# Transposing q by one crossbar DMA a batch, from batch 2 on, in a fused attention and GEGLU kernel

## The chip, the cores and the metric

One core of one Trainium2 chip. The metric is the device time of one execution in microseconds, the median over the runs named. Single executions of one kernel mostly agree within 0.2%, so differences of 0.5 us need several runs and a look at the trace.

## The reference, cut to what matters

```python
# q, k, v: (8 batches, 8 heads, 576 rows, 64); float32
q_s = softmax(q, axis=-1)            # over the 64 channels of a head
k_s = softmax(k, axis=2)             # over the 576 rows
kv  = einsum('bhsd,bhse->bhde', k_s, v)
x   = einsum('bhsd,bhde->bhse', q_s, kv)      # -> (4608 rows, 512 channels)
out = (gelu(x @ w_gate) * (x @ w_val)) @ w_out     # 512 -> 1536 -> 512
```

## The kernel before

Rows are worked in nine blocks: for each batch a block of 512 rows, and one more block of the 8 x 64 remainder rows. A block is twelve FFN tiles `FI` 0 to 11 (four matmuls for the gate, psg; four for the value, psv; gelu on ScalarE; the product ht on VectorE) and four row blocks `NS` 0 to 3 (twelve matmuls into psy each, then evacuation and store). The attention of batch b+1 rides along in block b: a plan says after which tile each piece is issued. In the program each engine has one list of instructions, worked in order (in run 9 VectorE stood 6.01 us at a sum with an evacuation, ready to run, behind it).

Names: eq and ek are the exp of q and k; q3 is q of batch 3, and so on. psg, psv, psy, psx, pst, pstr and pskv are the tiles in PSUM that TensorE writes: gate, value, output, x, transposes of the 512 rows and of the remainder rows, and kv. A bank is the place of one such tile; ps_big has six, ps_att two. The SP queue is SyncE's list of DMAs, issued one after the other (after the change: one from 69.56 us for 3.19, the next at 72.81). The chain is the profile's "chain of work that ended last", followed back from the last instruction.

For x = q_s · kv, the kernel's matmuls take q_s with channels on the partitions (`psx<-eqt,kv` in the trace). The kernel before makes that transpose in two ways. Batches 0 to 2: TensorE transposes into PSUM (8 transposes step by 0.50 us when nothing waits) and VectorE copies it out (0.68 us). Batches 3 to 7: VectorE transposes, in the 32x32 blocks of the code below (0.845 us a call), and 16 small DMAs move the blocks to their partitions (10.66 us of the SP queue in block 2).

```python
ps_big = tile_pool(name="ps_big", bufs=6, PSUM)    # psg, psv, psy, psx
ps_att = tile_pool(name="ps_att", bufs=2, PSUM)    # attention pieces
...
def unit_t(b, g, eng="dve"):                       # batches 0 to 2, twice a batch
    pst = ps_att.tile([P, 2, MAIN], f16, name="pst", tag="att")
    ... 8 x nc.tensor.transpose(pst[...], eq_b[b % 2][...], ident)
    ... copy to eqt on VectorE
def unit_t32(b, hp):                               # batches 3 to 7, four times a batch
    nc.vector.transpose(out=et[...], in_=eq_b[b % 2][...])
def moves(b):
    for a in range(4):
        for c in range(4):
            nc.sync.dma_start(out=t[32*c:32*c+32, a], in_=et[32*a:32*a+32, c])
...
at(1, FI, 3, L(exp, "q", 2), L(norm, 2, 0))        # softmax of q, batch 2
at(1, FI, 4, L(norm, 2, 1), L(unit_xrem, 1))
at(1, FI, 5, L(norm, 2, 2))
at(1, FI, 6, L(norm, 2, 3))
at(1, FI, 7, L(exp, "k", 2, 0, 4), L(cast_v, 2, 0, H))
at(1, FI, 9, L(unit_t, 2, 0))
at(1, FI, 10, L(unit_t, 2, 1))
at(1, FI, 11, L(load_batch, 3), L(exp, "k", 2, 4, 8), L(exp, "q", 3), L(exp, "k", 3), ...)
at(1, NS, 0, L(unit_trem, 2))                      # 4 more transposes: remainder rows
at(1, NS, 1, L(unit_kv4, 2))
at(1, NS, 2, L(unit_x4, 2, ("dve", "dve")))
```

The softmax here doesn't subtract the row's maximum and nothing guards it: scores larger than these inputs give would overflow.

## Time and profile before

| | before |
|---|---|
| time, median of 4 runs | 316.15 us (315.94 to 316.39) |
| span of the profiled execution | 314.5 us |
| TensorE / VectorE / ScalarE / GpSimd busy | 98 / 61 / 44 / 14% |
| start of block 2 on the chain | 85.42 us |
| length of blocks 2 and 3 | 33.42 and 32.89 us |

How to read it: matmuls overlap in the records (four 512-column ones are recorded as 1.03 us and start 0.86 us apart when nothing waits), so distances between starts are what to go by. The lines of TensorE in block 1 and of the chain are shown in the prediction.

### The profile page before, as it was taken

The page shows a single profiled execution, that of the slowest core. Times are in us where ns is not written, and L with a number is a line of the kernel's source. Part 1 is how long each engine was busy: PE and PEld are TensorE (multiplying, and loading weights), DVE is VectorE, ACT ScalarE, POOL GpSimd, SP SyncE. Part 2 cuts the span into 40 slices and gives each one's busy share as a digit, 9 for nine tenths or more (in the row PEclk, how much of TensorE's full clock was granted, in tenths as well). Part 3 has the DMA queues.
Part 4 walks back from the last instruction along what each step waited for, and adds up shares of the span by engine and source line. Part 5 has one row for each costly group of instructions (what it writes and reads, how often), then busy time and mean ns, then how long its engine had stood idle before and what let it go on. Part 6 is the DMA issues. An engine that isn't in the chain of part 4 may idle for free.

```text
span 314.5 us, 4799 instructions
## 1 busy us (share of the span) xinstructions
PE 307.7 (98%) x1826; PEld 143.7 (46%) x1826; DVE 191.1 (61%) x324; ACT 138.5 (44%) x178; POOL 44.7 (14%) x59
## 2 busy tenths in 40 slices
PE   8899999999999999999999999999999999999995
PEld 3444454444444444444444444444444444444443
DVE  3844386597898479746984599458943434324331
ACT  3753564988433663356334643374330233013300
POOL 2657451331001200030003000300000000000000
PEclk9999999999999999999999999999999999999999
DMA  7999999950178116921492139303021200140002
GB/s 231 372 383 394 401 386 388 395 194 0 69 245 306 53 70 194 349 59 67 127 386 80 72 90 383 115 27 131 1 58 28 115 18 0 35 101 0 3 33 100
DMA packets 42343, 50.78 MB, mean 161 GB/s; under 512 B 3408, under 2 KB 38096, under 8 KB 42320
## 3 DMA queue, kind: packets, MB, share of 16 engines
q1 hardware_dynamic: 40592, 48.84, 45.0%
q10 hardware_dynamic: 1728, 1.64, 1.6%
q8 instruction: 14, 0.23, 0.3%
q14 instruction: 9, 0.07, 0.1%
HBM read 37.75 MB, written 9.44 MB: 150 GB/s over the span
## 4 chain that ended last, share of the span: by engine, by line
PE 90%; DVE 4%; DMA 2%; ACT 2%; issue 1%; ACTq 0%; DVEq 0%
PE psy L489 29%; PE psg L411 28%; PE psv L411 27%; DMA qt<-in_q_dram 2%; PE pskv L284 1%; DVE eq L200 1%; PE psl L510 1%; PE psx L383 1%; DVE rq L191 1%; DVE rq L181 1%; DVE ht L418 1%; PE psx L365 1%; ACT eq L163 1%; PE pst L306 1%; ACT L416 0%
## 5 line engine op out<-in xcount | busy, mean ns | idle before, releaser
L416 ACT ACTIVATE gl<-psg 128x512 f32<-128x512 f32 x108 | 64.0, 599 | 131.0 <-PE psg L411 124.5
L418 DVE SCALAR_TENSOR_TENSOR ht<-psv,gl 128x512 f16<-128x512 f32 x108 | 72.9, 682 | 64.6 <-PE psv L411 64.1
L411 PE MATMUL psg<-xt,wg_sb 128*128 128x512 f16 x384 | 100.5, 379 | 0.1
L411 PE MATMUL psv<-xt,wv_sb 128*128 128x512 f16 x384 | 100.5, 379 | 0.0
L489 PE MATMUL psy<-wo_sb,ht 128*128 128x512 f16 x420 | 94.0, 379 | 0.0
L411 PEld LDWEIGHTS <-wv_sb 128*128 128x128 f16 x432 | 42.3, 98 | 51.2 <-issue 0.8
L411 PEld LDWEIGHTS <-wg_sb 128*128 128x128 f16 x432 | 41.9, 98 | 49.4 <-issue 0.4
L489 PEld LDWEIGHTS <-ht 128*128 128x128 f16 x420 | 40.4, 98 | 47.9 <-issue 0.8
L538 DVE TENSOR_SCALAR yo<-psy 128x512 f32<-128x512 f32 x30 | 20.5, 685 | 29.7 <-PE psy L489 29.7
L139 POOL CAST v<-vt 128x640 f16<-128x640 f32 x26 | 18.8, 763 | 137.1 <-DMA vt<-in_v_dram 98.3
L181 DVE TENSOR_REDUCE rq<-eq 128x10 f32<-128x640 f16 x28 | 22.7, 812 | 6.1 <-ACT eq L163 5.7
L200 DVE TENSOR_TENSOR eq<-eq,rrq 128x640 f16<-128x640 f16 (+1 forms) x29 | 23.7, 817 | 0.3
L163 ACT ACTIVATE ek<-kt 128x1280 f16<-128x1280 f32 (+1 forms) x11 | 19.1, 1746 | 3.4 <-DMA kt<-in_k_dram 3.3
L163 ACT ACTIVATE eq<-qt 128x2560 f16<-128x2560 f32 (+2 forms) x10 | 18.4, 1863 | 2.3 <-DMA qt<-in_q_dram 2.2
L331 DVE STREAM_TRANSPOSE et<-eq 128x640 f16<-128x640 f16 x20 | 16.9, 845 | 0.7
L411 PE MATMUL psg<-xtr,wg_sb 128*128 128x512 f16 x48 | 12.3, 379 | 0.0
L411 PE MATMUL psv<-xtr,wv_sb 128*128 128x512 f16 x48 | 12.3, 379 | 0.0
L143 DVE CAST xt<-psx 128x512 f16<-128x512 f32 x16 | 10.2, 682 | 1.2 <-PE psx L365 1.2
L403 PE MATMUL pswarm<-warm,ident 128*128 128x512 f16 x34 | 9.5, 438 | 1.4 <-POOL ident masks.py:199 1.4
L163 ACT ACT_TABLE_LOAD x8 | 10.3, 1283 | 0.6 <-DMA qt<-in_q_dram 0.5
L141 ACT CAST xt<-psx 128x512 f16<-128x512 f32 x16 | 8.7, 588 | 3.5 <-PE psx L365 3.5
L141 ACT CAST xtr<-psxr 128x128 f16<-128x128 f32 (+1 forms) x6 | 1.7, 283 | 17.8 <-PE psxr L383 17.8
(74 smaller groups left out, 122.6 us busy)
## 6 DMA issues: line engine op xcount, KB each, us to landing
out_dram<-yo SPq DMA_DIRECT2D x14, 512.0 KB, 3.5
kt<-in_k_dram SPq DMA_DIRECT2D x7, 640.0 KB, 7.9
vt<-in_v_dram SPq DMA_DIRECT2D x7, 640.0 KB, 8.4
qt<-in_q_dram SPq DMA_DIRECT2D x7, 640.0 KB, 6.5
qt<-in_q_dram SPq DMA_DIRECT2D x8, 512.0 KB, 6.7
eqt<-et SPq DMA_DIRECT2D x80, 40.0 KB, 1.9
wost<-in_moe_w_out_dram SPq DMA_DIRECT2D x6, 512.0 KB, 7.9
kt<-in_k_dram SPq DMA_DIRECT2D x6, 512.0 KB, 8.1
```

The source lines that it names most:

```text
L139: nc.gpsimd.tensor_copy(out=dst, in_=src)
L141: nc.scalar.copy(out=dst, in_=src)
L143: nc.vector.tensor_copy(out=dst, in_=src)
L163: nc.scalar.activation(out=dst[:, n0:NC, h0 * D:h1 * D].rearrange(o, d=D, **({"t": 2} if b >= QUAD else {})), in_=heads(tiles[(nm, b)], b, ...
L181: nc.vector.reduce_sum(rq, e, axis=mybir.AxisListType.X)
L200: (nc.gpsimd if eng == "pool" else nc.vector).tensor_tensor(out=e, in0=e, in1=rrq.unsqueeze(-1).to_broadcast((P, n, 2, D)), op=ALU.mult)
L331: nc.vector.transpose(out=et[:, :, hp].rearrange("p c (n i) -> p n c i", i=32), in_=eq_b[b % 2][:, :, hp * P:(hp + 1) * P].rearrange("p n ...
L411: nc.tensor.matmul(ps, w[:, ci, fi * P:(fi + 1) * P], xt[:, ci, :], start=(ci == 0), stop=(ci == HP - 1))
L416: nc.scalar.activation(out=gl, in_=psg, func=ACTF.Gelu)
L418: nc.vector.scalar_tensor_tensor(out=ht, in0=psv, scalar=_H_SCALE, in1=gl, op0=ALU.mult, op1=ALU.mult)
L489: nc.tensor.matmul(psy, hts[fi][:, ns * P:(ns + 1) * P], wo_sb[:, fi, :], start=(fi == 0), stop=(fi == NFI - 1))
L538: nc.vector.tensor_scalar(out=yo, in0=psy, scalar1=1.0 / _H_SCALE, scalar2=None, op0=ALU.mult)
```

## The change

Intent: take the transposes of batch 2 off TensorE, and for all later batches drop VectorE's block transposes and the 16 moves; one crossbar DMA does each batch (only my name for a DMA that transposes while it copies: `dma_start_transpose` in the code, DMA_TRANSPOSE in the profile). To have q of batch 2 ready earlier, its four multiplies go to GpSimd. kv and x of batch 2 come one row block earlier. The sums of batch 3 move from block 1 into block 2. With ps_att no longer used by transposes, FFN tile 7 of block 1 takes its two banks.

```diff
-    def unit_t32(b, hp): ...
-    def moves(b): ...
+    def unit_td(b):
+        t = att.tile([P, NC * C], f16, name="eqt", tag="eqt").rearrange(
+            "p (n h t) -> p n h t", n=NC, h=HP)
+        nc.sync.dma_start_transpose(out=t.rearrange("p n h t -> p (n h) t"),
+                                    in_=eq_b[b % 2].rearrange("p n c -> p (n c)"))
+        st[(b, "eqt4")] = t
 ...
-    def ffn_fi(xt, fi):
-        psg = ps_big.tile([P, 512], f32, name="psg", tag="mm")
+    def ffn_fi(xt, fi, spare=False):
+        pool, tag = (ps_att, "att") if spare else (ps_big, "mm")
+        psg = pool.tile([P, 512], f32, name="psg", tag=tag)
 ...                                   # psv the same
-    at(1, FI, 3, L(exp, "q", 2), L(norm, 2, 0))
+    at(1, FI, 3, L(exp, "q", 2), L(norm, 2, 0, "pool"))
 ...                                   # "pool" for the other three as well
-    at(1, FI, 9, L(unit_t, 2, 0))
-    at(1, FI, 10, L(unit_t, 2, 1))
+    at(1, FI, 9, L(unit_td, 2))
 ...
-    at(1, NS, 0, L(unit_trem, 2))
-    at(1, NS, 1, L(unit_kv4, 2))
-    at(1, NS, 2, L(unit_x4, 2, ("dve", "dve")))
+    at(1, NS, 0, L(unit_kv4, 2))
+    at(1, NS, 1, L(unit_x4, 2, ("dve", "dve")))
 ...                                   # batches n = b + 1 = 3 to 7:
-                at(b - 1, NS, hp, L(norm_sum, n, hp))
-                at(b, FI, hp, L(norm_mul, n, hp), L(unit_t32, n, hp))
-            at(b, FI, 4, L(moves, n))
+                at(*((b, FI, hp) if n == 3 else (b - 1, NS, hp)), L(norm_sum, n, hp))
+                at(b, FI, hp, L(norm_mul, n, hp))
+            at(b, FI, 4, L(unit_td, n))
 ...
-            hts.append(ffn_fi(xt, fi))
+            hts.append(ffn_fi(xt, fi, b == 1 and fi == 7))
```

More of the change, by code (lines that the diff above doesn't have):

```diff
@@ L103 @@
     QUAD = 2
-    T32 = 3
     def heads(x, b, h0, h1):
@@ L122 @@
     wst = {}
-    ETW = HP * 4 * NC * 32
     def wst_tile(name, n, w):
-        t = wstp.tile([P, ETW], f16, name=name, tag="wst")
-        return t[:, 0:2 * n * w].bitcast(f32).rearrange("p (n w) -> p n w", n=n)
+        return wstp.tile([P, HP * 256], f32, name=name, tag="wst")[:, 0:n * w].rearrange(
+            "p (n w) -> p n w", n=n)
     def load_w_gv(c):
@@ L295, in get_eqt @@
         if (b, "eqt") not in st:
-            st[(b, "eqt")] = att.tile([P, HP * 4 * NC * 32], f16, name="eqt", tag="eqt")[
+            st[(b, "eqt")] = att.tile([P, NC * C], f16, name="eqt", tag="eqt")[
                 :, 0:HP * S].rearrange("p (h t) -> p h t", h=HP)
@@ L324, in unit_trem @@
         nc.vector.tensor_copy(out=st[(b, "eqtr")], in_=pst[:, :, 0:REM] if b == 0 else pst[:, :, 0:P:2])
-    def unit_t32(b, hp):
-        if (b, "et") not in st:
-            st[(b, "et")] = wstp.tile([P, 4, HP, NC * 32], f16, name="et", tag="wst")
-        et = st[(b, "et")]
-        nc.vector.transpose(
-            out=et[:, :, hp].rearrange("p c (n i) -> p n c i", i=32),
-            in_=eq_b[b % 2][:, :, hp * P:(hp + 1) * P].rearrange("p n (c j) -> p n c j", j=32))
-    def moves(b):
-        t = att.tile([P, HP * 4 * NC * 32], f16, name="eqt", tag="eqt").rearrange(
-            "p (a h x) -> p a h x", a=4, h=HP)
-        for a in range(4):
-            for c in range(4):
-                nc.sync.dma_start(out=t[32 * c:32 * c + 32, a],
-                                  in_=st[(b, "et")][32 * a:32 * a + 32, c])
-        t = t.rearrange("p a h (n i) -> p h n a i", i=32)
-        st[(b, "eqt5")] = t
+    def unit_td(b):
[4 more added lines that the diff above has]
+        st[(b, "eqt4")] = t
     def xq(b, hp):
-        if (b, "eqt5") in st:
-            return st[(b, "eqt5")][:, hp, 1:NC]
+        if (b, "eqt4") in st:
+            return st[(b, "eqt4")][:, 1:NC, hp]
         return st[(b, "eqt")][:, hp, 0:MAIN]
     def xqr(b, hp):
-        if (b, "eqt5") in st:
-            return st[(b, "eqt5")][:, hp, 0, :, 0:32:2]
+        if (b, "eqt4") in st:
+            return st[(b, "eqt4")][:, 0, hp, 0:P:2]
         return st[(b, "eqtr")][:, hp, :]
@@ L420, in gate @@
         return ht
-    def ffn_fi(xt, fi):
-        psg = ps_big.tile([P, 512], f32, name="psg", tag="mm")
+    def ffn_fi(xt, fi, spare=False):
+        pool, tag = (ps_att, "att") if spare else (ps_big, "mm")
+        psg = pool.tile([P, 512], f32, name="psg", tag=tag)
         mm_gv(psg, wg_sb, xt, fi, range(HP))
-        psv = ps_big.tile([P, 512], f32, name="psv", tag="mm")
+        psv = pool.tile([P, 512], f32, name="psv", tag=tag)
         mm_gv(psv, wv_sb, xt, fi, range(HP))
@@ L630 @@
     at(1, FI, 2, L(unit_trem, 1))
-    at(1, FI, 3, L(exp, "q", 2), L(norm, 2, 0))
-    at(1, FI, 4, L(norm, 2, 1), L(unit_xrem, 1))
-    at(1, FI, 5, L(norm, 2, 2))
-    at(1, FI, 6, L(norm, 2, 3))
+    at(1, FI, 3, L(exp, "q", 2), L(norm, 2, 0, "pool"))
+    at(1, FI, 4, L(norm, 2, 1, "pool"), L(unit_xrem, 1))
+    at(1, FI, 5, L(norm, 2, 2, "pool"))
+    at(1, FI, 6, L(norm, 2, 3, "pool"))
     at(1, FI, 7, L(exp, "k", 2, 0, 4), L(cast_v, 2, 0, H))
-    at(1, FI, 9, L(unit_t, 2, 0))
-    at(1, FI, 10, L(unit_t, 2, 1))
+    at(1, FI, 9, L(unit_td, 2))
     at(1, FI, 11, L(load_batch, 3), L(exp, "k", 2, 4, 8), L(exp, "q", 3), L(exp, "k", 3), L(exp_rem0), L(cast_v, 3, 0, H))
-    at(1, NS, 0, L(unit_trem, 2))
-    at(1, NS, 1, L(unit_kv4, 2))
-    at(1, NS, 2, L(unit_x4, 2, ("dve", "dve")))
+    at(1, NS, 0, L(unit_kv4, 2))
+    at(1, NS, 1, L(unit_x4, 2, ("dve", "dve")))
     at(2, FI, 7, L(norm_rem0))
@@ L651 @@
             for hp in range(HP):
-                at(b - 1, NS, hp, L(norm_sum, n, hp))
-                at(b, FI, hp, L(norm_mul, n, hp), L(unit_t32, n, hp))
-            at(b, FI, 4, L(moves, n))
-            if n == T32:
+                at(*((b, FI, hp) if n == 3 else (b - 1, NS, hp)), L(norm_sum, n, hp))
+                at(b, FI, hp, L(norm_mul, n, hp))
+            at(b, FI, 4, L(unit_td, n))
+            if n == 3:
                 at(b, FI, 5, L(unit_kv4, n))
```

## The prediction

The forecast's sum came to -1.72 + 1.1 = -0.6 us, 315.3 us. The transpose's time in the SP queue, 5 us, and its landing 1.5 us after that were my estimates, which no trace showed. The times reckoned from them: q3 and k3 issued at 74.6 us, k3 landed at 82.9, transposed q landed at 76.1, the first gelu of block 2 started at 87.3 and its ht ended at 88.5. That is 1.1 us after the 87.4 that the text allows: the 1.1 of the sum. The 2.5 and 8 us under "The range" are other values for the same SP time, a factor of two about 5.

> **What bounds the kernel now.** I read the page's first rows, then its chain of work that ended last, then that chain in order of time, then the timelines of TensorE, ScalarE and the SP queue through block 1, where the change acts.
>
> ```profile
> PE 307.7 (98%) x1826; PEld 143.7 (46%) x1826; DVE 191.1 (61%) x324; ACT 138.5 (44%) x178; POOL 44.7 (14%) x59
> ```
> ```profile
> PE 90%; DVE 4%; DMA 2%; ACT 2%; issue 1%; ACTq 0%; DVEq 0%
> ```
>
> TensorE is busy for 98% of the span and 90% of the chain, and the pieces of the chain show that this is true throughput, not only overlapped records: from block 2 on, each group of four 512-column matmuls takes 0.86 us and each 12-matmul row block 2.6 us, with no gap. Blocks 3, 4 and 5 start at 151.73, 184.29 and 216.85 us, 32.56 apart; 24 x 0.864 + 48 x 0.216 = 31.1 of that is the FFN, the rest the two attention pieces (kv 0.75, x 0.63). So VectorE's 191 us are worth nothing by themselves. Only TensorE instructions taken out, or TensorE waits taken away, can shorten this kernel. TensorE in block 1 (start us, duration us, line, output, count):
>
> ```profile
> 59.51 1.03 PE L411 MATMUL psg<-xt,wg_sb 128*128 128x512 f16 x4
> 60.38 1.03 PE L411 MATMUL psv<-xt,wv_sb 128*128 128x512 f16 x4
> 61.24 1.03 PE L411 MATMUL psg<-xt,wg_sb 128*128 128x512 f16 x4
> 62.10 1.03 PE L411 MATMUL psv<-xt,wv_sb 128*128 128x512 f16 x4
> 63.21 1.02 PE L411 MATMUL psg<-xt,wg_sb 128*128 128x512 f16 x4
> ...
> 68.39 0.61 PE L306 MATMUL pst<-ident,eq 128*128 128x128 f16 x8
> 68.89 1.02 PE L411 MATMUL psg<-xt,wg_sb 128*128 128x512 f16 x4
> 69.75 1.03 PE L411 MATMUL psv<-xt,wv_sb 128*128 128x512 f16 x4
> 70.61 0.92 PE L306 MATMUL pst<-ident,eq 128*128 128x128 f16 x8
> 71.36 1.03 PE L411 MATMUL psg<-xt,wg_sb 128*128 128x512 f16 x4
> ...
> 75.68 0.39 PE L320 MATMUL pstr<-ident,eq 128*128 128x128 f16 x4
> 75.90 2.75 PE L489 MATMUL psy<-wo_sb,ht 128*128 128x512 f16 x12
> ```
>
> Read the distances between starts. 62.10 to 63.21 is 1.11 where 0.86 is the rule: a wait of 0.25. The first eight transposes cost 0.50, the second eight 0.75 (with a wait of about 0.3 for the last normalisation on VectorE), the four remainder ones 0.22. The waits-for view names the former: pst for DVE eq, 0.4 us.
>
> The wait at 63.21 comes from ScalarE, which had its tables changed twice around the exp of q2:
>
> ```profile
> 58.92 2.34 ACT L163 ACTIVATE eq<-qt 128x2560 f16<-128x2560 f32 x1
> 61.27 1.28 ACT L416 ACT_TABLE_LOAD   x1
> 62.56 0.60 ACT L416 ACTIVATE gl<-psg 128x512 f32<-128x512 f32 x1
> ```
>
> Tile 4 frees its bank at 63.16, and tile 7, three tiles later, needs that one of the six banks.
>
> [...] The trace has plain loads at 385 to 400 GB/s, no transposes. [...] the multiply at 69.85 us took 1.23 instead of 0.82 us while GpSimd cast.
>
> **The change part by part.**
>
> *TensorE.* Out go 16 + 4 transposes of batch 2: 0.50 + 0.75 + 0.22 = 1.47 us of start-to-start time, the wait for the last normalisation included. The spare banks for tile 7 of block 1 take away the wait of 0.25. Sum: **1.72 us**, all on the path. Batches 3 to 7 had no TensorE transposes, so nothing more comes from there: blocks 2 to 7 should keep 32.56 us each.
>
> *VectorE.* Out go 20 block transposes (20 x 0.845 = 16.9 us), two evacuations of 0.68, one of 0.41 and four multiplies of 0.82 (to GpSimd): some 22 us, off the path, worth nothing except where they delayed something.
>
> *GpSimd.* Four multiplies of 128x640. The one that it already does took 1.26 us, so 5.0 us. The sums on VectorE pace them: exp of q2 ends at 61.26; sum and reciprocal take 1.07, with a gate (0.65) between, so the four sums end at about 62.4, 64.9, 66.6 and 68.3, and the last multiply at **69.6**. The casts of v2 (4 x 0.72, before at 58.17) follow and end at 72.5.
>
> *The SP queue.* 80 moves of about 0.66 us issue time go; six transposes of 640 KB come. [...] For batches 3 to 7 this replaces 10.7 us of moves (start 96.90 in block 2) in a stage with need at 114.70: off the path.
>
> *Where it is on the path.* Batch 2's transpose waits in the SP queue for 69.6. Behind it, in order, stand the loads of batch 3, which before went out as soon as the queue was free:
>
> ```profile
> 52.69 1.34 SPq L117 DMA_DIRECT2D qt<-in_q_dram  x2
> 54.07 3.52 SPq L117 DMA_DIRECT2D kt<-in_k_dram  x2
> 60.92 1.28 SPq L117 DMA_DIRECT2D vt<-in_v_dram  x2
> ```
>
> [...] In block 2 the same two loads, issued from 87.85 into an idle DMA, had moved their 2.6 MB by about 96.1 (summing the GB/s of the one-microsecond windows): 8.3 us. [...] ScalarE then does exp k3 (2.32), the remainder exp (0.61) and the table load (1.28), all ahead of block 2's first gate[...].
>
> TensorE, 1.72 earlier, starts block 2 at 85.26 - 1.72 = 83.5. With six banks it can run three tiles ahead. The binding reader is VectorE: the sums of batch 3 have moved into block 2, so its first four tiles cost ht 0.6 + sum 0.81 + reciprocal 0.22 + multiply 0.82 = 2.45 each, against TensorE's 1.73. ht of tile 4 then ends 9.8 after ht of tile 0, and psv of tile 7 needs its bank at 83.5 + 0.86 + 7 x 1.73 + 0.75 (kv of batch 3) = 97.2. So ht of tile 0 may end as late as 87.4 without a stall[...]. The stall grows one for one with the transpose's SP time above 3.9 us.
>
> The x matmuls of batch 2, moved one row block earlier, would start at 82.03 - 2.70 - 1.72 = 77.6[...]. exp of the second half of k2, before at 75.6 and now about 74.0, is in time for kv of batch 2 at about 74.2, by little.
>
> Sum: -1.72 + 1.1 = -0.6 us, **315.3**.
>
> **The rivals.** *A: the clean gain.* The transpose issues in under 4 us, nothing stalls: 315.99 - 1.72 = 314.3. For it: the change puts the x matmuls one row block earlier, which nobody does whose transpose comes late; and the DMA stands idle (0 GB/s) between 68 and 80 us. Against it: the order of the SP queue. *B: the late loads.* The SP queue holds q3, k3 back, ScalarE waits at their exps with block 2's gates behind it, and TensorE runs out of banks. With 9 us of issue time the stall is 5.1: 319.4. For it: the removal of batch 3's sums from block 1's row blocks, which is what one does when exp q3 comes late. *C: the transpose itself is slow,* ten or more us of landing; then x of batch 2 waits too. Both waits overlap (one delay shifts the other's deadline), so with 12 us I would expect 12 - 3.9 - 1.72 = +6.4: 322.4. [...] *D: the DMA transposes hold the loads of later batches:* 18 us of slack per block speak against it.
>
> **The range.** The floor is A with small extras, 314.1. [...] 2.5 gives A, 8 gives 315.99 - 1.72 + 4.1 = 318.4. That makes 314.1 to 318.4 for 8 in 10. Faster by 2% needs 6.3 us off; only 1.72 can be had: 0.01. Slower by 2% needs about 12 us of SP time: 0.06. Within: 0.93.
>
> **What would show it.** In the profile after: TensorE's block 1 without pst and pstr, all steps 0.86; the GpSimd multiplies near 1.26 us; the transpose issued at about 69.6 [...]; q3 and k3 issued after it; ScalarE waiting for the k3 DMA[...]; and how long TensorE stands still in tiles 3 to 7 of block 2. Blocks 3 to 7 must keep 32.56. I am wrong if the loads are not behind the transpose[...], or if the later blocks change length.

## The result, and the profile after

| | before | after |
|---|---|---|
| time, median of 4 runs | 316.15 us | 314.74 us (314.71 to 314.79) |
| ratio to before, 95% interval | | 0.9955 (0.9938 to 0.9973) |
| span of the profiled execution | 314.5 us | 312.8 us |
| TensorE busy, instructions | 307.7 us, 1826 | 306.0 us, 1806 |
| VectorE busy | 191.1 us | 171.7 us |
| start of block 2 on the chain | 85.42 us | 83.80 us |
| length of block 2 on the chain | 33.42 us | 33.42 us |

A ratio is the mean time of one kernel's runs over that of the other's of the same rounds, so not quite the ratio of the medians. Where runs of different calls are compared below, I compare their ratios to before, or their traces.

The change is 1.4 us (0.45%) faster. First the page of the kernel after: engines, and the chain by engine.

```profile
PE 306.0 (98%) x1806; PEld 142.5 (46%) x1806; DVE 171.7 (55%) x297; ACT 138.5 (44%) x178; POOL 48.6 (16%) x63
...
PE 94%; DVE 2%; DMA 2%; ACT 0%; issue 0%; ACTq 0%
```

TensorE's share of the chain rises from 90 to 94%; ScalarE's 2% falls to 0. TensorE's timeline in block 1 of the kernel after (start us, duration us, line, output, count):

```profile
62.20 1.03 PE L397 MATMUL psv<-xt,wv_sb 128*128 128x512 f16 x4
63.06 1.03 PE L397 MATMUL psg<-xt,wg_sb 128*128 128x512 f16 x4
...
69.10 1.03 PE L397 MATMUL psv<-xt,wv_sb 128*128 128x512 f16 x4
69.97 1.03 PE L397 MATMUL psg<-xt,wg_sb 128*128 128x512 f16 x4
...
77.83 0.26 PE L369 MATMUL psxr<-eqt,kv 64*64 64x64 f16 x8
```

The step into psg of tile 7 is 63.06 - 62.20 = 0.86, so the wait of 0.25 us is gone; between tiles 10 and 11 stands nothing. x of batch 2 starts at 77.83, where I had 77.6, and waits for nothing. Next the SP queue of the kernel after:

```profile
69.56 3.19 SPq L327 DMA_TRANSPOSE eqt<-eq  x1
72.81 1.29 SPq L116 DMA_DIRECT2D qt<-in_q_dram  x2
74.15 1.31 SPq L116 DMA_DIRECT2D kt<-in_k_dram  x2
```

The transpose issues at 69.56 (I had 69.6) and q3 and k3 do stand behind it; but it holds SP for 3.19 us, where my estimate was 5. ScalarE, which needs these loads, in the kernel before and after:

```profile
75.51 2.32 ACT L163 ACTIVATE eq<-qt 128x2560 f16<-128x2560 f32 x1
```
```profile
79.12 2.34 ACT L160 ACTIVATE eq<-qt 128x2560 f16<-128x2560 f32 x1 [4.91 <-DMA qt<-in_q_dram]
82.07 2.34 ACT L160 ACTIVATE ek<-kt 128x2560 f16<-128x2560 f32 x1 [0.61 <-DMA kt<-in_k_dram]
...
86.23 1.09 ACT L402 ACTIVATE gl<-psg 128x512 f32<-128x512 f32 x2
```

The new wait is real: 4.91 us for q3 and 0.61 for k3, where the kernel before had none. Block 2's first gelu starts at 86.23, which is 2.59 us after the block's first matmul (83.64), where before it was 1.06 (86.32 after 85.26). It costs nothing, for block 2 is as long as before.

### The profile page after: what moved, and what is told of

It reads as the page before. It is cut to its first block, busy times and chain, and to the rows that moved or that the text cites. A ratio compares the mean times of both kernels' runs of the same rounds, so it can differ in the third digit from the quotient of the medians.

```text
span 312.8 us, 4653 instructions
## 1 busy us (share of the span) xinstructions
PE 306.0 (98%) x1806; PEld 142.5 (46%) x1806; DVE 171.7 (55%) x297; ACT 138.5 (44%) x178; POOL 48.6 (16%) x63
## 4 chain that ended last, share of the span: by engine, by line
PE 94%; DVE 2%; DMA 2%; ACT 0%; issue 0%; ACTq 0%
PE psg L397 30%; PE psv L397 30%; PE psy L476 29%; DMA qt<-in_q_dram 2%; PE pskv L281 1%; PE psl L497 1%; PE psx L369 1%; DVE rq L188 1%; PE psx L351 1%; DVE eq L197 0%; PE pst L303 0%; PE pskv L224 0%; PE psxr L369 0%; ACT eq L160 0%; PE pskv L258 0%; DVE v L140 0%
## 5 line engine op out<-in xcount | busy, mean ns | idle before, releaser
L404 DVE SCALAR_TENSOR_TENSOR ht<-psv,gl 128x512 f16<-128x512 f32 x108 | 73.8, 689 | 79.5 <-PE psv L397 75.0
L136 POOL CAST v<-vt 128x640 f16<-128x640 f32 x26 | 17.7, 724 | 115.0 <-DMA vt<-in_v_dram 105.4
L197 DVE TENSOR_TENSOR eq<-eq,rrq 128x640 f16<-128x640 f16 (+1 forms) x25 | 20.3, 813 | 0.3
L197 POOL TENSOR_TENSOR eq<-eq,rrq 128x640 f16<-128x640 f16 (+1 forms) x7 | 9.3, 1323 | 25.0 <-DVE rrq L180 17.3
```

Of the source, the lines that this page charges most:

```text
L136: nc.gpsimd.tensor_copy(out=dst, in_=src)
L197: (nc.gpsimd if eng == "pool" else nc.vector).tensor_tensor(out=e, in0=e, in1=rrq.unsqueeze(-1).to_broadcast((P, n, 2, D)), op=ALU.mult)
L404: nc.vector.scalar_tensor_tensor(out=ht, in0=psv, scalar=_H_SCALE, in1=gl, op0=ALU.mult, op1=ALU.mult)
```

## The experiments

Twelve kernels ran, in four calls; each call measured the kernel before anew on its chip. All gave correct results. The ratio of the changed kernel, to compare with, is 0.9955.

**1. Without the spare banks** (changed kernel).

```diff
-            hts.append(ffn_fi(xt, fi, b == 1 and fi == 7))
+            hts.append(ffn_fi(xt, fi))
```

> The changed kernel with tile 7 of block 1 back in the six FFN banks. My theory (the gain is 1.47 us of TensorE transposes and their wait, plus 0.25 us of bank wait): the step before psg of tile 7 grows again from 0.86 to about 1.1 us, the later starts of block 1 move by that, and since the slack before block 2's stall is close to nil, the time is 0.25 us above the changed kernel: about 315.0. Rival (the bank wait was hidden, or is moved to a later tile that waits anyway): the changed kernel's 314.74.

Measured: 314.95 us, ratio 0.9957 (0.9944 to 0.9969). The times alone don't tell it from the changed kernel. The trace does: psg of tile 7 starts at 63.17 after psv at 62.05, a step of 1.12 instead of 0.86 us, and from the first psg of tile 3 to block 2 it takes 83.74 - 55.89 = 27.85 us against 83.64 - 56.03 = 27.61. So the spare banks are worth 0.24 us, as expected.

**2. The spare banks alone** (kernel before).

```diff
-            hts.append(ffn_fi(xt, fi))
+            hts.append(ffn_fi(xt, fi, b == 1 and fi == 7))      # banks of ps_att
```

> The kernel before with only the spare banks for tile 7 of block 1. My theory: the wait of 0.25 us at psg of tile 7 goes; 0.25 us faster than before, about 315.9 against 316.15. Rival: the transposes of batch 2 wait for VectorE's last normalisation anyway, so the 0.25 us is given back in the wait of the second eight transposes, and the time stays at 316.15.

Measured: 317.19 us, ratio 1.0027 (1.0014 to 1.0040). Both theories miss: it is 0.9 us slower. From TensorE's timeline of this run:

```profile
71.84 0.61 PE L306 MATMUL pst<-ident,eq 128*128 128x128 f16 x8 [1.30 <-DVE ht L418]
```

The second eight transposes wait 1.30 us for an ht: they need a bank of ps_att, which tile 7 holds until its ht, and VectorE, busy with the normalisation, is late with that. The banks are spare only once the transposes have left. The two parts of the change are not additive.

**3. Crossbar for batches 3 to 7 alone** (block 1 as before).

```diff
 # changed kernel, with block 1's plan of the kernel before:
-    at(1, FI, 9, L(unit_td, 2))
+    at(1, FI, 9, L(unit_t, 2, 0))
+    at(1, FI, 10, L(unit_t, 2, 1))
 ...     # norms on VectorE, unit_trem, kv and x at NS 1 and 2, no spare banks, sums in block 1
```

> Block 1 as in the kernel before (TensorE transposes batch 2, no spare banks, sums of batch 3 in block 1); only batches 3 to 7 go through the crossbar, so VectorE loses 17 us of block transposes and the SP queue 80 moves. My theory: nothing on the path, so the time of before, 316.15 within 0.2. Rival (the relief of VectorE or of the SP queue is what pays): most of the 1.4 us gain, about 314.9.

Measured: 316.10 us, ratio 0.9992 (0.9978 to 1.0006): the kernel before.

**4. Crossbar for batches 2 and 3 alone.**

```diff
-            at(b, FI, 4, L(unit_td, n))
+            at(b, FI, 4, L(unit_td if n == 3 else moves, n))    # and unit_t32 for n > 3
```

> The changed kernel, but batches 4 to 7 transposed as before on VectorE with 16 moves each. My theory: block 1 alone pays, so the changed kernel's 314.74 within 0.2. Rival (VectorE relief pays): about 1 us slower, near 315.8.

Measured: 314.54 us, ratio 0.9943 (0.9930 to 0.9955): the changed kernel. Runs 3 and 4 together show where the gain sits: in the part of the change that acts in block 1, and not in the five batches whose block transposes and 80 moves went away.

**5. A second, unused transpose ahead of the loads.**

```diff
+    dum = const.tile([P, NC * C], f16)
 ...
         st[(b, "eqt4")] = t
+        if b == 2:
+            nc.sync.dma_start_transpose(out=dum[:, 0:2560]..., in_=eq_b[0]...)
```

> The changed kernel with a second, unused crossbar transpose of the same 640 KB queued right behind that of batch 2, ahead of the loads of batch 3. My theory: SP needs 3.2 us more, q3 and k3 issue and land 3.2 us later, block 2's first gelu starts at about 89.4 and TensorE stalls by the 3.2 us less the slack of about 0.1: 314.74 + 3.1 = 317.8, all of it in tiles 3 to 7 of block 2. Rival (there is slack that I do not see, for instance because VectorE's work in block 2 is not the deadline): under 1 us slower.

Measured: 317.40 us (one run of four 318.67), ratio 1.0032 (1.0015 to 1.0048), 0.8% or 2.4 us above the changed kernel. The second transpose took SP 3.15 us; q3's exp starts 3.2 us later (82.29), k3's 4.1 us later (86.20), and the first gelu at 90.37. TensorE's timeline in block 2 of the profiled run, the one of 318.67 us:

```profile
91.02 1.02 PE L402 MATMUL psg<-xt,wg_sb 128*128 128x512 f16 x4 [2.02 <-ACT gl L407]
91.88 1.83 PE L402 MATMUL psv<-xt,wv_sb 128*128 128x512 f16 x4
93.50 1.91 PE L402 MATMUL psg<-xt,wg_sb 128*128 128x512 f16 x4
```

The loads do stall TensorE, as the theory says. But the place is another: psg of tile 3 waits for the gelu of tile 0. That gelu came 4.1 us late, and 2.0 us of it became a wait: so some 2 us of slack had been there, not 0.1. The matmuls after it are slow for another reason, in the windows view (last columns: granted clock, DMA share, GB/s):

```profile
91.00:92.00 1.00, 0.98 (x5) 0.48 (x5) 1.00 (x2) 0.95 (x2) 1.00 (x2) 0.98 1.06 388
92.00:93.00 1.00, 1.00 (x4) 0.30 (x2) 0.86 (x3) 0.60 (x1) 0.05 (x1) 0.50 1.09 385
...
95.00:96.00 1.00, 1.00 (x5) 0.41 (x4) 0.94 (x2) 0.55 (x1) 0.00 (x0) 0.82 1.08 387
```

After standing for 2 us, TensorE was granted half its clock from about 92.0, for about 3.4 us, which cost another 1.7 us: block 2's psy starts at 109.10 against 105.22, 3.9 in all. The other three runs, with a mean clock of 1.000, 1.000 and 0.998, are at 317.07 to 317.57.

**6. Half of it.** As 5, with 10 of the 20 blocks.

```diff
-            nc.sync.dma_start_transpose(out=dum[:, 0:2560]..., in_=eq_b[0]...)
+            nc.sync.dma_start_transpose(out=dum[:, 0:1280]..., in_=eq_b[0]...[:, 0:1280])
```

> As the run with the full second transpose, but the unused one has 10 of the 20 blocks. My theory: SP time in proportion, so 1.6 us later loads and a stall of 1.5 us: 316.2. If the time of a transpose is mostly fixed: nearly as slow as the full one, 317.5. If there is hidden slack: 314.8.

Measured: 315.95 us, ratio 0.9988 (0.9974 to 1.0003), 1.0 us above the changed kernel. The transpose of ten blocks took SP 1.39 us and that of twenty 3.15, so its time grows with size. First gelu at 88.69, 2.5 us late. TensorE's waits in block 2:

```profile
89.34 1.02 PE L402 MATMUL psg<-xt,wg_sb 128*128 128x512 f16 x4 [0.39 <-ACT gl L407]
...
100.08 1.02 PE L402 MATMUL psv<-xt,wv_sb 128*128 128x512 f16 x4 [0.23 <-DVE ht L409]
```

Here both limits show, each at its edge: 0.39 us at psg of tile 3, and 0.23 at psv of tile 8 for the ht of tile 4. Psy of block 2 starts 106.12 - 105.22 = 0.9 us later. That runs 5 and 6 came near the 317.8 and 316.2 expected is luck in part: k3 fell 0.8 to 1.0 us further back than I reckoned, and the slack was 1.5 to 2 us and not 0.1.

**7. The second transpose, with q3 and k3 queued first.**

```diff
-    at(1, FI, 9, L(unit_td, 2))
+    at(1, FI, 9, L(load_batch, 3, ((q, "q"), (k, "k"))), L(unit_td, 2))
 ...
-    at(1, FI, 11, L(load_batch, 3), ...
+    at(1, FI, 11, L(load_batch, 3, ((v, "v"),)), ...
```

> The full second transpose again, but the loads of q3 and k3 are queued ahead of the first transpose (v3 stays behind). My theory (the stall comes through the loads): q3 and k3 issue near 53 us, ScalarE never waits for them, no stall: 314.7. Rival (the second transpose itself hurts, through the DMA engines or by holding v3 and the stores): still about 317.8.

Measured: 314.93 us, ratio 0.9957 (0.9942 to 0.9972): the changed kernel's time, although batch 2's transpose is made twice. ScalarE's exp q3 starts at 74.24, the first gelu of block 2 at 84.82. So the loss of run 5 comes through the order of the SP queue and not through the transposing itself.

**8. Batch 2's multiplies back on VectorE.**

```diff
-    at(1, FI, 3, L(exp, "q", 2), L(norm, 2, 0, "pool"))
+    at(1, FI, 3, L(exp, "q", 2), L(norm, 2, 0))         # and the other three
```

> The changed kernel with the four multiplies of batch 2 back on VectorE. My theory: the last one ends at about 71.0 instead of 69.5, so the transpose, q3 and k3 come 1.5 us later and block 2 stalls by about 1.4 us: 316.1. Rival (the deadline is not real, or the move to GpSimd was worth nothing): 314.8.

Measured: 315.45 us, ratio 0.9973 (0.9958 to 0.9988), 0.6 us above the changed kernel. It is slower, but not by the mechanism that I named. The transpose issues at 70.96 and the first gelu of block 2 starts at 88.51, 2.3 us later than in the changed kernel (1.65 us later within block 2, which itself starts 0.63 later, at 84.27), and yet block 2 has no wait at all. The loss is in block 1:

```profile
72.15 2.75 PE L476 MATMUL psy<-wo_sb,ht 128*128 128x512 f16 x12 [0.24 <-ACT gl L402]
74.83 1.01 PE L281 MATMUL pskv<-v,ek 128*64 128x65 f16 x40
75.77 2.76 PE L476 MATMUL psy<-wo_sb,ht 128*128 128x512 f16 x12
```

Psy waits for a late gelu (1.27 after the psv at 70.88 instead of 0.86), and kv steps 0.94 instead of 0.75: ScalarE's last gelus waited 1.47 us for VectorE's ht, and with them the exp of k2's second half, which ends at 75.27, while kv runs. Together 0.6. It is the multiplies on VectorE, not the loads.

**9. The sums of batch 3 back in block 1.**

```diff
-                at(*((b, FI, hp) if n == 3 else (b - 1, NS, hp)), L(norm_sum, n, hp))
+                at(b - 1, NS, hp, L(norm_sum, n, hp))
```

> The changed kernel with the sums of batch 3 back in the row blocks of block 1. My theory: VectorE meets the first sum right after the first row block's evacuation and waits in order for exp q3 until about 81.5, so the x evacuations of batch 2 end near 86 instead of 81.4, TensorE's block 2 starts 2 to 3 us late, part of which is won back because block 2's VectorE chain is 1.03 us a tile shorter: 316.5 to 317.5. Rival (the order does not matter): 314.8.

Measured: 318.74 us (318.89, 318.59, 319.22, 316.68), ratio 1.0065 (1.0037 to 1.0093). VectorE, then TensorE, in this run:

```profile
81.78 0.82 DVE L178 TENSOR_REDUCE rq<-eq 128x10 f32<-128x640 f16 x1 [6.01 <-ACT eq L160]
```
```profile
83.51 4.03 PE L476 MATMUL psy<-wo_sb,ht 128*128 128x512 f16 x12 [2.42 <-DVE yo L525]
```

VectorE stands 6.01 us at a sum whose q3 has not come, and TensorE 2.42 us for the evacuation behind it. The run of 316.68 us, at a mean clock of 1.000, I take to hold the wait alone (no trace of it was kept): 1.9 us above the changed kernel's 314.74, in the expected range. The three others have a mean clock of 0.994 or 0.995; in the profiled one it fell to 0.50 from 85 to 88 us.

**10. Going on: remainder rows of batches 0 and 1 by crossbar as well.**

```diff
+    def unit_tdrem(b):
+        t = att.tile([P, HP, P], f16, name="eqtr", tag="eqtr", bufs=2)
+        nc.sync.dma_start_transpose(out=t, in_=eq0r if b == 0 else eq_b[1][:, 0, :])
+        st[(b, "eqtr")] = t[:, :, 0:REM] if b == 0 else t[:, :, 0:P:2]
 ...
-    at(1, FI, 2, L(unit_trem, 1))
+    at(1, FI, 2, L(unit_tdrem, 1))      # its x (unit_xrem) at FI 9 instead of FI 4
-    at(3, FI, 8, L(unit_trem, 0))
+    at(3, FI, 5, L(unit_tdrem, 0))
```

> A try to go on: the changed kernel with the remainder rows of batches 1 and 0 also transposed by small crossbar DMAs (4 blocks each), so that 8 TensorE transposes and two evacuations go. My theory (TensorE instructions taken out pay one for one): 0.22 us each, 0.44 us in all, 314.3. Rival: block 2's VectorE deadline has no slack left, so the 0.22 us won in block 1 comes back as a stall in block 2, and only the 0.22 of block 3 is won: 314.5. It also gives a second size for the crossbar's SP time: 4 blocks, about 0.64 us if in proportion, more if part of it is fixed.

Measured: 314.13 us, ratio 0.9932 (0.9918 to 0.9945), span 312.3 against 312.8. The interval overlaps the changed kernel's, 0.9938 to 0.9973, but run 12 repeats it, and the traces account for it: block 2 starts at 83.51 instead of 83.80 us on the chain, and block 3 lasts 116.93 to 149.60 = 32.67 instead of 117.22 to 150.12 = 32.90. In both places four transposes of 0.22 us are gone; that is 0.44 of the 0.5 us between the two spans. The small transposes of 4 blocks held SP for 1.39 and 1.27 us, both while other transfers ran (388 and 336 GB/s in those fortieths of the span).

**11. kv and x of batch 2 at their old places.**

```diff
-    at(1, NS, 0, L(unit_kv4, 2))
-    at(1, NS, 1, L(unit_x4, 2, ("dve", "dve")))
+    at(1, NS, 1, L(unit_kv4, 2))
+    at(1, NS, 2, L(unit_x4, 2, ("dve", "dve")))
```

> The changed kernel with kv and x of batch 2 at their old places, one row block later each. If the move is worth nothing by itself: 314.74, x at about 81.2 in the trace and no wait before block 2. If it is needed (x's four evacuations of 2.5 us on VectorE then end only at block 2's start): a wait at the first psg of block 2 of up to 0.5 us, 315.2.

Measured: 314.75 us, ratio 0.9950 (0.9937 to 0.9962): no difference. This part of the change is worth nothing by itself.

**12. Version 10 with q3 and k3 queued first.** The edit of run 7, on the version of run 10.

> The version with the remainder rows of batches 0 and 1 on the crossbar, and q3 and k3 queued ahead of batch 2's transpose. The changed kernel has about 2 us of slack at block 2 by the runs so far, so the earlier loads should win nothing: the time of the version without them, a ratio of 0.993 to before (314.1). If they win more than 0.3 us, some stall in block 2 was not seen. First gelu of block 2 at about 84.5 instead of 86.2.

Measured: 314.07 us, ratio 0.9931 (0.9917 to 0.9944). First gelu of block 2 at 84.37. As fast as version 10, so block 2 held no hidden stall there. With version 10 it is the fastest here, 2.2 us below the kernel before, and q3 and k3 don't stand behind the transpose.

## Why the prediction was right, and where not

I predicted 315.3 (314.1 to 318.4); measured 314.74. The time lies in the range, but on the path of rival A, the clean gain (314.3): what block 1 wins came, and the stall of 1.1 us in block 2, which sets 315.3 apart from A, did not. Three slips in the text: 315.99 - 1.72 + 1.1 is 315.4; twice my 5 us is 10, where the range stops at 8; and its "blocks 3, 4 and 5" are blocks 4, 5 and 6. Only blocks 4 and 5 take 32.56 us; blocks 2 and 3 took 33.42 and 32.89 before, and 33.42 and 32.90 after. The steps:

- **TensorE is the bound; only its instructions and its waits count: right.** Runs 3 and 4 show it: 17 us of VectorE work and 80 moves are worth nothing (run 3: ratio 0.9992). Later blocks keep their length. But VectorE's four multiplies in block 1 are worth 0.6 us, through TensorE's waits (run 8).
- **1.72 us gained in block 1: right.** From the first psg of tile 3 to block 2 it takes 83.64 - 56.03 = 27.61 us, before 85.26 - 55.94 = 29.32: 1.71 less. (In time it is 1.4 us, by the ratio's interval 0.9 to 2.0.) The spare banks' share of it is 0.24 (run 1). What I did not see: that share exists only without the transposes (run 2). The transposes' 1.47 was not tried alone; it rests on the steps in the two traces, with runs 3 and 4.
- **GpSimd's pace: right.** The four multiplies took 1.26 us each, the last ended at 69.5, and the casts of v2 at 72.2.
- **5 us of SP time for the transpose: too large.** That was an estimate of mine which nothing in the trace showed. Measured 3.19 us, and the data landed 5.0 us after the issue, where I had 6.5. The bytes took about 3 us (last section). I had named a time far from 5 us as a sign that I am wrong, and by that this was a miss.
- **Loads of batch 3 behind the transpose: right,** and so is the chain behind them. k3's exp began at 82.07 (I had 82.9) and the first gelu at 86.23 (87.3); with the transposes' real time the rest of the chain is off by 0.7.
- **"psv of tile 7 needs its bank" from the ht of tile 4: wrong.** This is the step that failed; with the 5 us it made the 1.1 us stall. I assumed that six banks go round in order, so that a tile's psv follows the psv three tiles before. The program as built hands a bank on as it comes free, and a psg is free earlier than its psv. The banks of ps_big (0 to 5) in block 2, read from the built program of the changed kernel:

```
tile   0  1  2  3  4  5  6  7  8
psg    0  1  3  0  5  0  5  0  5
psv    5  4  2  1  3  4  2  1  3
```

Psv of tile 7 has bank 1, last held by psv of tile 3; psv of tile 8 has bank 3, after tile 4. So the chain of 2.45 us a tile has one tile more. In the changed kernel's trace (the first line holds the ht of tiles 4 and 5, the second is psv of tile 8):

```profile
97.01 1.28 DVE L404 SCALAR_TENSOR_TENSOR ht<-psv,gl 128x512 f16<-128x512 f32 x2
```
```profile
99.17 1.03 PE L397 MATMUL psv<-xt,wv_sb 128*128 128x512 f16 x4
```

The ht of tile 4 ended at about 97.65: 1.5 us to spare, and with my bank rule psv of tile 7, which began at 97.45, would have had to wait 0.2. Psg of tile 3 follows the gelu of tile 0, which ended at about 86.8; it began at 88.8: 2.0. Run 8, whose first gelu came 1.65 us later within block 2, had no wait there, run 6, with 2.5 us, met both limits, and run 12 gained nothing: the slack is shown.

The stall needed both errors. With the right banks my own 5 us give none: the ht of tile 4 would end at 88.5 + 9.8 = 98.3, before psv of tile 8 at 97.2 + 1.73 = 98.9. And with my banks 3.19 us lie below the 3.9 from which the stall was to grow (by the trace, a wait of 0.2 us). Rival B (late loads) is real but was not reached: it appears once the first gelu comes 2.5 us later (run 6). C and D did not show: x waited for nothing, and the later blocks kept their length. And I had no step for what comes after a stall: half the clock for over 3 us, which nearly doubled the loss in the profiled execution of run 5.

Left open: why k3 fell 0.8 to 1.0 us further behind q3 in runs 5, 6 and 8 than in the changed kernel.

## What to carry to other kernels

When one engine is saturated (here TensorE, 98% busy), count only what leaves it and the waits that it loses, and put each part of a change to the test alone: here 20 transposes in one block paid, and five batches of the same edit paid nothing. A DMA that waits for data holds the loads behind it in its queue (here q3 was issued at 72.81 us, and at 52.93 in run 7 with the loads first), so put loads that are ready ahead of it (314.93 us in run 7 against 317.40 in run 5), and reckon how late they may land. To reckon that, take the bank order from the built program and not from a rule of rotation.

## What the runs show of the transposing DMA, the clock and the banks

- Time in the SP queue: a transpose of 640 KB took 3.19 us with no load beside it, and one of half of that 1.39 us (run 6). Beside loads, the same instruction held SP for up to 6.77 us (changed kernel, at 158.69 us, while the DMA moved 312 GB/s).
- Rate: with nothing else to move, the transpose of batch 2 moved 198 to 217 GB/s at a full DMA share (windows view; last columns granted clock, DMA share, GB/s), while plain loads moved 389 and 401 (kernel before, windows 20 to 30 and 30 to 40 us; no plain SBUF copy of this size ran). With the 24 KB of the microsecond before, these three make its 655 KB:

```profile
71.00:72.00 1.00, 1.00 (x6) 0.48 (x5) 0.45 (x2) 0.95 (x2) 1.00 (x2) 1.00 1.15 215
72.00:73.00 1.00, 1.00 (x7) 0.41 (x6) 0.66 (x1) 0.99 (x2) 0.20 (x1) 1.00 1.17 217
73.00:74.00 1.00, 1.00 (x6) 0.48 (x5) 0.00 (x0) 1.00 (x1) 0.00 (x0) 1.00 1.07 198
```

- Clock: in the profiled executions of runs 5 and 9 TensorE stood for 2.0 and 2.4 us. The granted clock fell to half 0.9 and 1.3 us after the matmuls had begun again, and stayed there for about 3.4 us (by the mean clocks, in one execution of four of run 5 and three of four of run 9). That the standing was the cause is argued from this order; no run tried it.
- Banks: the tile pool of the program as built hands PSUM banks on in another order than round. In tiles 5 to 8 of block 2, psv follows the psv four tiles before and psg the psg two before.
